# Order of the first loads of a SwiGLU feed-forward kernel: everything on SyncE's queue, x in two pieces

## The chip, the cores and the metric

The kernel runs on one core of a Trainium2 chip. The metric is the device time of one execution in microseconds. Three runs of the kernel before gave 120.56, 121.11 and 121.32 us, so its median is 121.11 us. One more execution was taken with the hardware profiler; all views below are of that one.

## The reference

```python
B, S, D, F = 1, 2048, 512, 1376          # bf16 throughout
def reference(x, w_gate, w_up, w_down):
    g = jax.nn.silu(x @ w_gate)          # [2048, 512] @ [512, 1376]
    u = x @ w_up
    return (g * u) @ w_down              # [2048, 1376] @ [1376, 512]
```

## The kernel before

TensorE (PE) contracts over partitions, so x is needed with D on the partitions: the tile xT_sb holds x transposed, four blocks of 128 of D by 2048 tokens. Tokens go in four chunks of 512. F is cut into ten full tiles of 128 columns and a rest of 96. For each chunk and each F tile PE makes a gate product and an up product (four matmuls each, one per block of D, out to one PSUM bank of 128x512, line 327). ScalarE (ACT) takes SiLU of the gate bank into sg_sb (line 279), VectorE (DVE) multiplies it with the up bank into hT_sb (line 288). After all chunks PE makes the down product from hT_sb and the w_down tile wd_sb (line 392), DVE copies each row block to o_sb (line 292), and SyncE (SP) stores it. The rest of 96 columns has matmuls of its own (lines 368, 379 and 406).

The work of every engine is one list written out by hand; semaphores join them. PE's list sets the order. Each matmul group waits, through need(name), for the loads that it reads, and through after(engine, n) for the n-th operation of ACT or DVE.

The change touches the start alone, which runs like this.

- **Transposed x.** Chunks 1 to 3 and the second half of chunk 0 (tokens 256 to 511, the load x0b) come through transposing DMAs straight into xT_sb (line 86). The first 256 tokens come as a plain load, xn (line 107), into xn_sb, and PE transposes them: two token tiles i = 0, 1, each in two halves h = 0, 1 of D, each half two 128x128 transposes (line 344) into its own PSUM bank. DVE copies the halves h = 0 to xT_sb, ACT the halves h = 1. Here tile i holds every second token, since xn puts two neighbouring tokens on one partition; rows_of undoes this when the output rows are stored.
- **Loads.** ACT issues the gate and the up weights of F tile 0 ahead of its first work (line 91). SP issues xn, the gate and up weights of F tile 1, x0b, and then the rest in slabs of F tiles (2, 3), (4 to 6), (7 to the end), the other chunks of x, and w_down.
- **PE.** Five dummy matmuls of 512 columns on constants (line 336, N_WARM) run first. Then PE waits for the identity and for xn, makes the eight transposes, and then, for F tiles 0 and 1 of chunk 0 (gate g0, up u0, gate g1, up u1): g0 on tokens 0 to 127, g0 on 128 to 255, u0 likewise, g1 and u1 on tokens 0 to 255, and then all four on tokens 256 to 511, which need x0b. From F tile 2 on every matmul has 512 columns.

Of the kernel before, what the change touches and what calls it, by code (L numbers as in the profile page):

```python
# [7 lines left out]
FP32 = mybir.dt.float32  # L8

N_WARM = 5  # L10


def bass_standalone__swiglu_ffn__prompt_kernel(nc, x, w_gate, w_up, w_down, out):
    _, S, D = x.shape
    F = w_gate.shape[1]
    P = 128
    KD = D // P
    NFF = F // P
    NFT = NFF + 1
# [8 lines left out]
    HT = SC // 2  # L28
    NXN = HT // P
# [5 lines left out]
    xf = x[0]  # L35
    of = out[0]


    UPH = F + 32
# [4 lines left out]
    with ExitStack() as es:  # L44
# [16 lines left out]
        o_sb = [sb(f"o_sb{i}", [P, D], BF16) for i in range(NOS)]  # L61
        banks = [ps(f"bank{i}", [P, 512], FP32) for i in range(NB)]

        xn_sb = sb("xn_sb", [P, NXN, D], BF16)
# [8 lines left out]
        s_out = [sem(f"s_out{i}") for i in range(NOS)]  # L73
        loads = {}

        def load_sem(name):
            loads[name] = sem(f"s_{name}")
            return loads[name]
# [6 lines left out]
        def load_x(eng, name, t0, t1):  # L85
            eng.dma_start_transpose(
                xT_sb[:, :, t0:t1], xf[t0:t1, :]
            ).then_inc(load_sem(name), 16)

        def load_w(eng, name, src, base, f0, f1):  # L90
            eng.dma_start(
                w_sb[:, :, base + f0:base + f1],
                src[:, f0:f1].rearrange("(k p) f -> p k f", p=P),
            ).then_inc(load_sem(name), 16)

        slabs = [(0, 1), (1, 2), (2, 4), (4, 7), (7, NFT)]
        slab_of = {ft: a for a, b in slabs for ft in range(a, b)}

        def load_slab(eng, a, b):
            load_w(eng, f"wg{a}", w_gate, 0, a * P, min(b * P, F))  # L100
            load_w(eng, f"wu{a}", w_up, UPH, a * P, min(b * P, F - 32))

        def loads_on_scalar(act):
            load_slab(act, *slabs[0])

        def loads_on_sync(sp):
            sp.dma_start(
                xn_sb[:, :, :].rearrange("p j d -> p (j d)"), xf[0:HT, :].rearrange("(p j) d -> p (j d)", j=NXN)
            ).then_inc(load_sem("xn"), 16)
            load_slab(sp, *slabs[1])  # L110
            load_x(sp, "x0b", HT, SC)
            for a, b in slabs[2:]:
                load_slab(sp, a, b)
            load_w(sp, "wut", w_up, F - (F - 32), F - 32, F)
            for c in range(1, NSC):
                load_x(sp, f"x{c}", c * SC, (c + 1) * SC)
            sp.dma_start(
                wd_sb[:, 0:NFF, :], w_down[0:NFF * P, :].rearrange("(k p) d -> p k d", p=P)
            ).then_inc(load_sem("wd"), 16)
            for c in range(NSC):  # L120
                sp.dma_start(
                    wdt_sb[R * c:R * (c + 1), :, :], w_down[NFF * P:F, :].rearrange("(q p) d -> p q d", p=R)
                ).then_inc(load_sem(f"wdt{c}"), 16)
            sp.dma_start(wdl_sb[:, :], w_down[NFF * P:F, LASTA:D]).then_inc(load_sem("wdl"), 16)
# [7 lines left out]
        def add_group(kind, **what):  # L132
            g = dict(kind=kind, at=len(groups), bank=banks[len(groups) % NB], readers=[], **what)
            groups.append(g)
            return g
# [8 lines left out]
        def tview(bank):  # L144
            return bank[:, 0:P].bitcast(BF16).rearrange("p (k t) -> p k t", k=2)
# [61 lines left out]
        for i in range(NXN):  # L207
            for h, eng in enumerate("DA"):
                g = add_group("T", i=i, h=h)
                op = add_op(  # L210
                    eng, g, kind="copy", out=xT_sb[:, 2 * h:2 * h + 2, i * P:(i + 1) * P],
# [15 lines left out]
        for at in range(NST):  # L227
            j, c = divmod(at, NSC)
            t = c * TPC + j
            ob = at % NOS  # L230
            need = 16 * n_store[ob]
            halves = [(0, D)] if at < NST - 1 else [(0, LASTA), (LASTA, D)]
            for c0, c1 in halves:
                g = add_group("O", t=t, c0=c0, c1=c1, c=c)
                if c0 == 0:
                    quads[j].append(g)
                else:
                    last = g
                eng = "A" if len(halves) == 2 and c0 == 0 else "D"
                op = add_op(  # L240
                    eng, g, kind="copy", out=o_sb[ob][:, c0:c1], src=g["bank"][:, 0:c1 - c0],
# [3 lines left out]
                n_store[ob] += 1  # L245


        def rows_of(t):
            if t < NXN:
                return of[0:HT, :].rearrange("(p j) d -> j p d", j=NXN)[t]  # L250
            return of[t * P:(t + 1) * P, :]

        def on_sync(sp):
            loads_on_sync(sp)
            for t, c0, c1, ob, eng, n in stores:
                sp.wait_ge(s_A if eng == "A" else s_D, n)
                sp.dma_start(rows_of(t)[:, c0:c1], o_sb[ob][:, c0:c1]).then_inc(s_out[ob], 16)
            for i in range(NOS):
                sp.wait_ge(s_out[i], 16 * n_store[i])

# [3 lines left out]
            ).then_inc(s_I, 1)  # L264

        def on_scalar(act):
            loads_on_scalar(act)
            act.activation(adummy[:, 0:4], zero_c, ACT.Silu)  # L268
            for op in act_ops:
                act.wait_ge(s_P, op["g"]["at"] + 1)  # L270
                if op["kind"] == "silu":
                    if op["free"]:
                        act.wait_ge(s_D, op["free"])
                    fn = ACT.Silu
                else:
                    if op["stored"][1]:
                        act.wait_ge(*op["stored"])
                    fn = ACT.Copy
                act.activation(op["out"], op["src"], fn).then_inc(s_A, 1)  # L279
# [15 lines left out]
        def on_tensor(pe):  # L295
            landed = set()

            def need(name):
                if name not in landed:
                    pe.wait_ge(loads[name], 16)  # L300
                    landed.add(name)
# [3 lines left out]
            def after(eng, n):  # L305
                if n > read[eng]:
                    pe.wait_ge(s_A if eng == "A" else s_D, n)
                    read[eng] = n
# [6 lines left out]
            def gu_matmuls(g, n0, n1):  # L315
                c, ft = g["c"], g["ft"]
                if c > 0:
                    need(f"x{c}")
                if c == 0 and n1 > HT:
                    need("x0b")  # L320
                need(("wg" if g["kind"] == "G" else "wu") + str(slab_of[ft]))
                col = (0 if g["kind"] == "G" else UPH) + ft * P
                for dk in range(KD):
                    if c == 0 and dk % 2 == 0:
                        for i in range(n0 // P, min(n1 // P, NXN)):
                            after(*xt_ready[i, dk // 2])
                    ins = pe.matmul(  # L327
                        g["bank"][:, n0:n1], lhsT=w_sb[:, dk, col:col + P],
                        rhs=xT_sb[:, dk, c * SC + n0:c * SC + n1], start=(dk == 0), stop=(dk == KD - 1),
                    )  # L330
                if n1 == SC:
                    ins.then_inc(s_P, 1)

            def warm(n, width):
                for i in range(n):
                    pe.matmul(banks[NB - 1][:, 0:width], lhsT=ones_w, rhs=ones_m[:, 0:width], start=True, stop=True)  # L336

            warm(N_WARM, SC)
            pe.wait_ge(s_J, 1)
            need("xn")  # L340
            for g in groups[:NT]:
                for k in range(2):
                    dk = 2 * g["h"] + k
                    ins = pe.transpose(tview(g["bank"])[:, k, :], xn_sb[:, g["i"], dk * P:(dk + 1) * P], ident[:, :])  # L344
                ins.then_inc(s_P, 1)

            g0, u0, g1, u1 = groups[NT:NT + 4]
            for g in (g0, u0):
                gu_matmuls(g, 0, P)
                gu_matmuls(g, P, HT)  # L350
            gu_matmuls(g1, 0, HT)
            gu_matmuls(u1, 0, HT)
            for g in (g0, u0, g1, u1):
                gu_matmuls(g, HT, SC)
# [73 lines left out]
            t, c0, c1 = last["t"], last["c0"], last["c1"]  # L428
# [3 lines left out]
            ).then_inc(s_P, 1)  # L432

        on_sync(nc.sync)
        on_gpsimd(nc.gpsimd)
        on_scalar(nc.scalar)
        on_tensor(nc.tensor)
        on_vector(nc.vector)

# [27 lines left out]
```

## Time and profile before

| | us |
|---|---|
| median of three runs | 121.11 |
| the profiled execution | 120.31 |
| its span, first to last instruction | 119.0 |
| PE busy | 115.6 (97%) |
| DVE busy | 47.2 (40%) |
| ACT busy | 31.0 (26%) |
| first transpose on PE | 3.71 |
| first matmul of line 327 | 4.56 |

A PE that is busy need not run at its best: the records of matmuls overlap, so the spacing of their starts tells the speed. A matmul of 512 columns starts every 0.216 us in the long middle part of this kernel, and every 0.427 us among the first dummies. An instruction that issues a DMA is listed under its engine with a q (SPq, ACTq) and its time is that of issuing; the time to landing runs from the start of the issue until the semaphore has its full count.

### The profile page before, as it was taken

Reading aid. Unit: us, or ns where it says so; the run is one execution under the profiler, and the core shown is the slowest. Engines: PE = TensorE matmul, PEld = TensorE weight load, DVE = VectorE, ACT = ScalarE, POOL = GpSimd, SP = SyncE. Lnnn points to the kernel's source line nnn. Section 1 sums busy time; section 2 is a strip of 40 time slices with the busy share of each in tenths; the row PEclk is TensorE's granted clock in tenths of the full one; section 3 lists DMA queues with packets and bytes.
Section 4 is the critical chain, followed back from the end, with each engine's and each line's share of the span. In section 5 each row is a group of like instructions: output and inputs, shape, how many; then the busy total and the mean of one; then the engine's idle time right before and its main releaser. Section 6 shows DMA issues by size and latency. Waiting matters only on the chain.

```text
span 119.0 us, 1524 instructions
## 1 busy us (share of the span) xinstructions
PE 115.6 (97%) x608; PEld 53.7 (45%) x608; DVE 47.2 (40%) x73; ACT 31.0 (26%) x53; POOL 0.4 (0%) x5
## 2 busy tenths in 40 slices
PE   7799999999999999999999999999999999999993
PEld 1674444444444444444444444444434444444452
DVE  0133443353433444433444334469617422006530
ACT  4344324453234363244262343230000000000001
POOL 1000000000000000000000000000000000000000
PEclk9999999999999999999999999999999999999999
DMA  3999999990000000000000000000004221002412
GB/s 90 277 299 365 265 101 272 307 254 10 0 0 0 6 0 0 0 0 6 0 0 0 6 0 0 0 0 0 0 0 138 88 88 44 0 0 76 150 44 88
DMA packets 17559, 8.84 MB, mean 74 GB/s; under 512 B 10640, under 2 KB 17424, under 8 KB 17552
## 3 DMA queue, kind: packets, MB, share of 16 engines
q1 hardware_dynamic: 16496, 8.48, 27.8%
q10 hardware_dynamic: 1056, 0.26, 1.0%
q8 instruction: 5, 0.08, 0.3%
q14 instruction: 2, 0.02, 0.0%
HBM read 4.81 MB, written 2.10 MB: 58 GB/s over the span
## 4 chain that ended last, share of the span: by engine, by line
PE 95%; DMA 2%; DVE 0%; issue 0%
PE bank L327 58%; PE bank L392 29%; PE bank L368 3%; DMA xn_sb<-in_x_dram 2%; PE bank L406 2%; PE bank L379 2%; PE bank L344 1%; DVE o_sb L292 0%; PE bank L429 0%
## 5 line engine op out<-in xcount | busy, mean ns | idle before, releaser
L327 PE MATMUL bank<-xT_sb,w_sb 128*128 128x512 bf16 (+2 forms) x344 | 70.0, 364 | 0.0
L327 PEld LDWEIGHTS bank<-xT_sb,w_sb 128*128 128x128 bf16 x344 | 32.8, 98 | 36.3
L288 DVE TENSOR_TENSOR hT_sb<-sg_sb,bank 128x512 bf16<-128x512 f32 x40 | 27.5, 688 | 40.4 <-PE bank L327 36.6
L392 PE MATMUL bank<-wd_sb,hT_sb 128*128 128x512 bf16 (+2 forms) x170 | 35.1, 367 | 0.0
L279 ACT ACTIVATE sg_sb<-bank 128x512 f32<-128x512 f32 x40 | 23.8, 596 | 40.7 <-PE bank L327 40.7
L392 PEld LDWEIGHTS bank<-wd_sb,hT_sb 128*128 128x128 bf16 x170 | 16.0, 98 | 19.1 <-issue 1.3
L292 DVE CAST o_sb<-bank 128x512 bf16<-128x512 f32 (+1 forms) x16 | 10.1, 663 | 22.0 <-PE bank L406 12.3
L279 ACT ACTIVATE o_sb<-bank 128x384 bf16<-128x384 f32 x1 | 0.5, 490 | 37.8 <-PE bank L392 37.8
L288 DVE TENSOR_TENSOR ht_sb<-sgy_sb,bank 32x512 bf16<-32x512 f32 x8 | 5.5, 683 | 0.2
L288 DVE TENSOR_TENSOR ht_sb<-sgx_sb,bank 32x512 bf16<-32x512 f32 x4 | 2.8, 692 | 3.5 <-ACT sgx_sb L279 3.5
L368 PE MATMUL bank<-xT_sb,w_sb 128*128 128x512 bf16 x16 | 4.1, 379 | 0.0
L279 ACT ACTIVATE sgx_sb<-bank 32x512 f32<-32x512 f32 x4 | 2.3, 587 | 4.5 <-PE bank L368 4.5
L336 PE MATMUL bank<-const-bfloat16-1.0 128*128 128x512 bf16 x5 | 2.3, 621 | 0.8 <-PEq L452 0.8
L406 PE MATMUL bank<-wdt_sb,ht_sb 32*128 32x512 bf16 (+1 forms) x48 | 2.9, 372 | 0.0
L368 PEld LDWEIGHTS bank<-xT_sb,w_sb 128*128 128x128 bf16 x16 | 1.6, 98 | 1.9
L279 ACT ACTIVATE sgy_sb<-bank 64x512 f32<-64x512 f32 x4 | 2.4, 590 | 0.1
L379 PE MATMUL bank<-xT_sb,w_sb 128*64 128x512 bf16 x16 | 1.9, 382 | 0.0
L406 PEld LDWEIGHTS bank<-wdt_sb,ht_sb 32*128 32x128 bf16 x48 | 1.1, 92 | 1.7 <-issue 0.8
L268 ACT ACT_TABLE_LOAD x1 | 1.3, 1283 | 1.8 <-issue 1.8
L292 DVE COPY xT_sb<-bank 128x256 bf16<-128x256 bf16 x2 | 0.6, 292 | 2.9 <-PE bank L344 2.8
L344 PE MATMUL bank<-ident,xn_sb 128*128 128x128 bf16 x8 | 0.8, 275 | 0.6 <-DMA xn_sb<-in_x_dram 0.6
L344 PEld LDWEIGHTS bank<-ident,xn_sb 128*128 128x128 bf16 x8 | 0.7, 130 | 1.5 <-issue 1.5
(14 smaller groups left out, 4.0 us busy)
## 6 DMA issues: line engine op xcount, KB each, us to landing
out_dram<-o_sb SPq DMA_DIRECT2D x15, 128.0 KB, 1.7
wd_sb<-in_w_down_dram SPq DMA_DIRECT2D x1, 1280.0 KB, 8.0
w_sb<-in_w_gate_dram SPq DMA_DIRECT2D x1, 480.0 KB, 6.0
w_sb<-in_w_up_dram SPq DMA_DIRECT2D x1, 448.0 KB, 6.6
w_sb<-in_w_gate_dram SPq DMA_DIRECT2D x1, 384.0 KB, 4.7
w_sb<-in_w_up_dram SPq DMA_DIRECT2D x1, 384.0 KB, 5.2
wdt_sb<-in_w_down_dram SPq DMA_DIRECT2D x4, 96.0 KB, 6.8
xn_sb<-in_x_dram SPq DMA_DIRECT2D x1, 256.0 KB, 2.8
```

The costliest lines, as they stand in the source:

```text
L268: act.activation(adummy[:, 0:4], zero_c, ACT.Silu)
L279: act.activation(op["out"], op["src"], fn).then_inc(s_A, 1)
L288: ins = dve.tensor_tensor(op["out"], op["a"], op["b"], ALU.mult)
L292: ins = dve.tensor_copy(op["out"], op["src"])
L327: ins = pe.matmul(g["bank"][:, n0:n1], lhsT=w_sb[:, dk, col:col + P], rhs=xT_sb[:, dk, c * SC + n0:c * SC + n1], start=(dk == 0), stop=(dk ...
L336: pe.matmul(banks[NB - 1][:, 0:width], lhsT=ones_w, rhs=ones_m[:, 0:width], start=True, stop=True)
L344: ins = pe.transpose(tview(g["bank"])[:, k, :], xn_sb[:, g["i"], dk * P:(dk + 1) * P], ident[:, :])
L368: ins = pe.matmul(g["bank"][:, :], lhsT=w_sb[:, dk, XC0:XC0 + P], rhs=xT_sb[:, dk, c * SC:(c + 1) * SC], start=(dk == 0), stop=(dk == KD - 1),
L379: ins = pe.matmul(g["bank"][y0:y1, :], lhsT=w_sb[:, dk, YC0:YC0 + 64], rhs=xT_sb[:, dk, c * SC:(c + 1) * SC], start=(dk == 0), stop=(dk == ...
L392: ins = pe.matmul(g["bank"][:, 0:c1 - c0], lhsT=hT_sb[:, fk, t * P:(t + 1) * P], rhs=wd_sb[:, fk, c0:c1], start=(start and fk == 0), stop= ...
L406: ins = pe.matmul(g["bank"][:, 0:c1 - c0], lhsT=ht_sb[R * c:R * (c + 1), q, j * P:(j + 1) * P], rhs=wdt_sb[R * c:R * (c + 1), q, c0:c1], s ...
```

## The change

- All early loads are issued by SP, none by ACT. Their order is: piece 0 of x (128 tokens, xn0), the gate weights of F tiles 0 and 1 in one load (wg0, 256 columns), piece 1 of x (xn1), the up weights of both tiles in one load (wu0), then x0b and the slabs as before.
- The pieces of x are plain tiles of 128 tokens, so rows_of goes away.
- PE runs two dummies of 128 columns more ahead of the wait (N_FILL), waits for each piece of x by itself, and runs four dummies of 128 columns (N_WAIT) between the transposes of piece 0 and the wait for piece 1.
- The first matmuls are reordered: g0 and g1 on tokens 0 to 127, g0 and g1 on tokens 128 to 255, u0 and u1 on tokens 0 to 255, then all four on tokens 256 to 511.

```diff
+N_FILL = 2
+N_WAIT = 4
...
-        slabs = [(0, 1), (1, 2), (2, 4), (4, 7), (7, NFT)]
+        slabs = [(0, 2), (2, 4), (4, 7), (7, NFT)]
...
-        def loads_on_scalar(act):
-            load_slab(act, *slabs[0])
+        def load_xn(eng, i):
+            eng.dma_start(xn_sb[:, i, :], xf[i * P:(i + 1) * P, :]).then_inc(load_sem(f"xn{i}"), 16)
 
         def loads_on_sync(sp):
-            sp.dma_start(
-                xn_sb[:, :, :].rearrange("p j d -> p (j d)"), xf[0:HT, :].rearrange("(p j) d -> p (j d)", j=NXN)
-            ).then_inc(load_sem("xn"), 16)
-            load_slab(sp, *slabs[1])
+            load_xn(sp, 0)
+            load_w(sp, "wg0", w_gate, 0, 0, slabs[0][1] * P)
+            load_xn(sp, 1)
+            load_w(sp, "wu0", w_up, UPH, 0, slabs[0][1] * P)
             load_x(sp, "x0b", HT, SC)
-            for a, b in slabs[2:]:
+            for a, b in slabs[1:]:
                 load_slab(sp, a, b)
...
-        def rows_of(t):
-            if t < NXN:
-                return of[0:HT, :].rearrange("(p j) d -> j p d", j=NXN)[t]
-            return of[t * P:(t + 1) * P, :]
...
         def on_scalar(act):
-            loads_on_scalar(act)
             act.activation(adummy[:, 0:4], zero_c, ACT.Silu)
...
             warm(N_WARM, SC)
+            warm(N_FILL, P)
             pe.wait_ge(s_J, 1)
-            need("xn")
             for g in groups[:NT]:
+                if g["i"] > 0 and g["h"] == 0:
+                    warm(N_WAIT, P)
+                need(f"xn{g['i']}")
                 for k in range(2):
...
             g0, u0, g1, u1 = groups[NT:NT + 4]
-            for g in (g0, u0):
-                gu_matmuls(g, 0, P)
-                gu_matmuls(g, P, HT)
-            gu_matmuls(g1, 0, HT)
+            for n0, n1 in ((0, P), (P, HT)):
+                gu_matmuls(g0, n0, n1)
+                gu_matmuls(g1, n0, n1)
+            gu_matmuls(u0, 0, HT)
             gu_matmuls(u1, 0, HT)
             for g in (g0, u0, g1, u1):
                 gu_matmuls(g, HT, SC)
```

More of the change, by code (lines that the diff above doesn't have):

```diff
@@ L256, in on_sync @@
                 sp.wait_ge(s_A if eng == "A" else s_D, n)
-                sp.dma_start(rows_of(t)[:, c0:c1], o_sb[ob][:, c0:c1]).then_inc(s_out[ob], 16)
+                sp.dma_start(of[t * P:(t + 1) * P, c0:c1], o_sb[ob][:, c0:c1]).then_inc(s_out[ob], 16)
             for i in range(NOS):
```

## The prediction

> **What bounds the kernel now.** I read the chain that ended last first, since it tells in which stretch a change can count at all.
>
> ```profile
> 0.74 2.83 DMA xn_sb<-in_x_dram
> 3.58 0.14 issue
> 3.71 0.85 PE bank L344 x8
> 4.56 17.66 PE bank L327 x104
> ...
> 23.08 17.27 PE bank L327 x80
> ```
>
> Columns: start, length, what. From 3.71 us to 117 us the chain is PE alone, so the end moves only by what moves PE's start or opens a hole behind it. The first chunk's 104 matmuls hold the columns of the 80 in a later chunk and take 17.66 - 17.27 = 0.39 us more. Second, the issues in order of time and the times to landing (last number).
>
> ```profile
> 0.73 0.46 ACTq L91 DMA_DIRECT2D w_sb<-in_w_gate_dram  x1
> 0.74 0.39 SPq L107 DMA_DIRECT2D xn_sb<-in_x_dram  x1
> 1.19 0.41 SPq L91 DMA_DIRECT2D w_sb<-in_w_gate_dram  x1
> ...
> 2.20 1.77 SPq L86 DMA_TRANSPOSE xT_sb<-in_x_dram  x1
> 4.02 0.58 SPq L91 DMA_DIRECT2D w_sb<-in_w_gate_dram  x1
> ```
>
> ```profile
> xn_sb<-in_x_dram SPq DMA_DIRECT2D x1, 256.0 KB, 2.8
> w_sb<-in_w_gate_dram SPq DMA_DIRECT2D x1, 256.0 KB, 3.5
> w_sb<-in_w_up_dram SPq DMA_DIRECT2D x1, 256.0 KB, 3.7
> w_sb<-in_w_up_dram SPq DMA_DIRECT2D x1, 128.0 KB, 3.8
> out_dram<-o_sb SPq DMA_DIRECT2D x15, 128.0 KB, 1.7
> ```
>
> xn lands at 0.74 + 2.83 = 3.57 and the first transpose starts 0.13 later. The last up load ahead of x0b lands at 1.66 + 3.8 = 5.4. The same list cut to 2 to 4 us gives x0b 4.2 us, so it lands at 6.4. The matmuls that need it start at 6.49: **x0b has 0.05 us to spare**. Third, the busy times by stretch (PE, PEld, DVE, ACT, POOL, granted clock, DMA share, GB/s).
>
> ```profile
> 0.77:3.06 2.29, 2.29 (x5) 0.55 (x5) 0.23 (x1) 1.28 (x1) 0.23 (x1) 1.00 0.47 129
> 3.06:3.71 0.65, 0.00 (x1) 0.03 (x1) 0.00 (x0) 0.21 (x2) 0.00 (x0) 1.00 1.23 277
> ...
> 1.75:2.50 0.75, 0.75 (x4) 0.15 (x1) 0.00 (x0) 0.72 (x1) 0.00 (x0) 1.00 0.68 145
> 2.50:3.50 1.00, 0.56 (x2) 0.00 (x0) 0.00 (x0) 0.77 (x2) 0.00 (x0) 1.00 1.09 307
> 3.50:4.75 1.25, 1.04 (x10) 0.83 (x10) 0.56 (x2) 0.42 (x2) 0.00 (x0) 1.00 1.28 286
> 4.75:5.75 1.00, 1.00 (x18) 0.92 (x17) 0.03 (x1) 0.24 (x1) 0.00 (x0) 1.00 1.29 273
> ```
>
> PE's hole of 0.65 us lies between dummies and transposes, and the DMA engines are full from 2.5 us on: what is asked for first comes first, and the rest waits for bytes. The clock column says 1.00 throughout, but transposes start 0.107 us apart up to 4.2 us and 0.055 us apart after 4.3, so PE doubles its speed near 4.25 us.
>
> **Piece 0 of x.** xn0 is half of xn and issued at the same 0.74. Bounds for its landing: 2.44 (the 128 KB store's 1.7 us) and 3.57 (nothing gained). 128 KB less at 307 GB/s is 0.4 us, so I take 3.2. The dummies end at 3.06 + 2 x 0.107 = 3.27. Transposes of piece 0: from 3.33, four at 0.107, to 3.76. The four waiting dummies: to 4.19. All this gains nothing by itself, since PE then waits for piece 1.
>
> **Piece 1 of x decides.** Ahead of xn1's last byte stand xn0, wg0 and xn1: 512 KB (524 thousand bytes). Before, the engines had moved 0.75 x 145 = 109 by 2.50, 109 + 307 = 416 by 3.50, and 524 at 3.5 + 108/286 = 3.88. Semaphores follow the bytes: 768 KB (786) were through at 4.75 + 13/273 = 4.80 and the last up load landed at 5.4, a lag of 0.6. So xn1 lands near 4.45. Its own issue agrees: xn0 takes SP to 1.19, wg0 some 0.5 to 1.69, and 1.69 + 2.8 (xn's row) = 4.49. Low end: 415 thousand bytes after 2.50 at the 365 GB/s of the page's fourth slice (8.9 to 11.9 us, rows of 768 bytes and more), 3.64, with a lag of 0.4: 4.05. High end: wg0 lands 3.5 after its issue at 1.19 as the row of 256 KB does, 4.69, and xn1 another 131/307 = 0.4 later: 5.1. I take 4.45, on which two ways agree.
>
> **The first matmuls.** Before, the last transpose started at 4.34 and the x0b matmuls at 6.49, 2.15 later; that held three waits for copies of transposes, read from the starts (0.217, 0.158 and 0.098 us apart where 0.055 is the pace): 0.16 + 0.10 + 0.04 = 0.30 us. In the new order piece 0 is copied long before, so the first two waits go. Piece 1's ACT copy was ready 5.05 - 4.34 = 0.71 after the last transpose; now 0.055 + 8 x 0.056 + 2 x 0.056 = 0.62 lies in front of the matmul that needs it: a wait of 0.09. Gain 0.30 - 0.09 = 0.2 us. Matmul count and columns stay (104).
>
> So, with xn1 at L: transposes from L + 0.13, the last at L + 0.30, the x0b matmuls at L + 0.30 + 2.15 - 0.21 = L + 2.24. **Break-even with 6.49 is L = 4.25.** With 4.45: +0.2 us. Ends: 4.05 gives -0.2, 5.1 gives +0.85.
>
> **The other loads.** wu0 closes the same 768 KB, so 5.4; it is wanted at L + 1.3 = 5.8 (nothing; issued at 2.14, its 3.7-us row gives 5.84, also next to nothing). x0b's bytes again come behind 768 KB, but its issue moves from 2.20 to about 2.68, since SP now carries two 256-KB weight loads and one x issue more in place of two of 128 KB. Bound by bytes it lands at 6.4 and hides before 6.69. Bound by its issue it lands at 2.68 + 4.2 = 6.9: 0.2 us. I take bytes: the engines show no free share ahead of it. The DMA row first (two queues, together 286 GB/s), then the rule: by the Trainium skill, "DMA: Bandwidth & Descriptors", section "Issuing engines are not separate DMA queues", a second issuing engine saves only issue time, no bandwidth. That speaks against this change: it would give that saving up, and by it x0b is at 6.4 while bytes bind and at 6.9 where issuing does; no run shown here tells which.
>
> Later slabs move by 0.5 us in issue: (2, 3) landed at 4.02 + 3.5 = 7.5 and is wanted at 8.24, so the cover holds even then. ACT loses two issues and loads its table earlier, ending at 3.06 now and first needed at 4.33: nothing. The plain output rows are the same 128 KB stores.
>
> **The clock.** The two and four dummies shrink the hole of 0.65 us. PE sped up 3.5 us after its first dummy in spite of that hole, so nothing is gained in this execution. The three timed runs lie 0.25 to 1.0 us above it; if that is a later rise of the clock (each microsecond later costs half of it), a denser start might bring some of it forward. Bounds: 0 and 0.8 us (all of the median's excess, 121.11 - 120.31); I take 0.1, near the end that the row shows.
>
> **Sum.** 120.31 + 0.2 - 0.1 = 120.4 us for an execution like the profiled one. The median stands 0.8 above, so 121.11 + 0.1 = **121.2 us, no change that can be told**: about 1%, or 1.2 us, is what a measurement of this kernel can tell.
>
> **The rivals.**
> - *Bytes come sooner and the clock earlier.* Larger pieces run faster (L = 4.05, -0.2) and the filled hole gives back half of the excess (-0.4): 120.5 us. For it: 256-byte rows become 512-byte rows, 308 GB/s where those of 512 bytes flow (6.5 to 7.75) against 286. Against: the clock rose despite the hole. Chance 0.22.
> - *SP's queue is the new limit: slower.* wg0 and xn1 are bound by issue and latency, not bytes: L = 5.1, x0b matmuls at 7.34 (x0b at 6.9 already there): +0.85, 121.9 to 122.0. It decides once L passes 4.25, and shows as a PE hole ahead of piece 1's transposes, which dummies end too early to cover (4.19). For it: one sequencer issues what two did. Against: bytes flowed at 273 to 307 GB/s from 2.5 us on, so issue was ahead of them. Chance 0.18.
> - *It does not bring x forward.* The first 1.0 us to the first bytes is fixed and xn0 lands at 3.57: transposes to 4.13, dummies to 4.56, piece 1 then from 4.56, L in effect 4.43: as forecast, 121.2. It is counted there.
> - *The clock is a matter of phase.* Row: speed doubles at 4.25. If it can rise anywhere within the next 3.4 us, each run has its own cold stretch and filling changes nothing: up to 1.7 us on single runs, 121.3 at the median (the +0.2 alone). The rule beside it: the Trainium skill, "TensorE: Matmul & The Clock Gate", Part 1, has a free-running window of 3413 ns. The trace agrees with its length (3.5 us after the first dummy); one execution cannot show its phase. Chance 0.15.
>
> **How the numbers follow.** Forecast 0.45, rivals 0.22, 0.18 and 0.15. The forecast and the phase rival lie within 1%. Faster by over 1% means under 119.9, the first rival with all of the 0.8: 0.08. Slower by over 1% means over 122.3, the second with a later clock: 0.10. The rest, 0.82, is within. The range reaches to both outer rivals, 120.4 to 122.0.
>
> **What would show it.** In the profile after: first transpose near 3.3; the second four near 4.6, with a DMA wait of xn_sb of 0.3 to 0.4 us ahead of them; the starts behind without the gaps of 0.217 and 0.158; x0b matmuls near 6.7 and unbroken; x0b's time to landing down to about 3.7 to 3.9. The forecast falls if x0b or wu0 ends a wait of PE for over 0.3 us, if piece 1 starts before 4.2 or after 5.1, or if the middle chunks (17.27 us) change.

## The result and the profile after

The kernel after takes 121.37 us at the median of 20 runs (121.15 to 121.56); the kernel before, run 20 times beside it, 120.62 us (120.30 to 121.90). The ratio, formed over all runs (the two medians alone give 1.006), is 1.0043, 95% interval 1.0026 to 1.0059: slower by 0.4%, within the 1% that was called no change. The profiled execution took 121.54 us, its span is 120.1 us; before it was 120.31 and 119.0.

The chain of work that ended last in the kernel after (start, length, what):

```profile
1.66 0.50 SPq L106
2.16 0.04 issue
2.20 4.33 DMA w_sb<-in_w_up_dram
6.53 0.04 issue
6.58 2.96 PE bank L323 x24
```

Before, the chain came to PE at 3.71 us by way of xn. Now it runs through SP's own issues and the up load wu0, which takes 4.33 us from its issue and holds PE until 6.58.

SP's issues of the kernel after in order of time, and PE's work beside them:

```profile
0.74 0.40 SPq L106 DMA_DIRECT2D xn_sb<-in_x_dram  x1
1.20 0.41 SPq L93 DMA_DIRECT2D w_sb<-in_w_gate_dram  x1
1.66 0.50 SPq L106 DMA_DIRECT2D xn_sb<-in_x_dram  x1
2.20 0.43 SPq L93 DMA_DIRECT2D w_sb<-in_w_up_dram  x1
2.68 1.57 SPq L88 DMA_TRANSPOSE xT_sb<-in_x_dram  x1
```

```profile
3.07 0.63 PE L343 MATMUL bank<-ident,xn_sb 128*128 128x128 bf16 x4
3.50 0.63 PE L332 MATMUL bank<-const-bfloat16-1.0 128*128 128x128 bf16 x4
4.60 0.61 PE L343 MATMUL bank<-ident,xn_sb 128*128 128x128 bf16 x4 [0.47 <-DMA xn_sb<-in_x_dram]
5.00 1.39 PE L323 MATMUL bank<-xT_sb,w_sb 128*128 128x128 bf16 x16
6.58 1.65 PE L323 MATMUL bank<-xT_sb,w_sb 128*128 128x256 bf16 x12 [0.18 <-DMA w_sb<-in_w_up_dram]
```

The transposes of piece 0 start at 3.07, of piece 1 at 4.60, the first matmul at 5.00 (4.56 before), the first on wu0 at 6.58. The matmuls that need x0b start at 7.61 in the trace, 6.49 before. That is 1.12 us, and the span grew by 1.1: all that was lost was lost ahead of this point.

The stretches that tell why (PE, PEld, DVE, ACT, POOL, granted clock, DMA share, GB/s), first of the kernel after, then of the kernel before:

```profile
2.50:3.00 0.50, 0.50 (x4) 0.23 (x3) 0.00 (x0) 0.00 (x0) 0.00 (x0) 1.00 0.71 131
3.00:4.00 1.00, 1.00 (x11) 0.86 (x9) 0.29 (x1) 0.26 (x1) 0.00 (x0) 1.00 1.04 308
4.00:6.50 2.50, 1.93 (x22) 1.62 (x20) 0.29 (x1) 0.51 (x2) 0.00 (x0) 1.00 1.04 170
```

```profile
2.50:3.00 0.50, 0.50 (x2) 0.00 (x0) 0.00 (x0) 0.50 (x1) 0.00 (x0) 1.00 0.97 333
3.00:4.00 1.00, 0.35 (x5) 0.32 (x5) 0.00 (x0) 0.27 (x2) 0.00 (x0) 1.00 1.24 284
4.00:6.50 2.50, 2.50 (x32) 2.02 (x31) 0.58 (x2) 0.66 (x2) 0.00 (x0) 1.00 1.21 264
```

From 4.0 to 6.5 us the DMA engines moved 170 GB/s in place of 264. Their share did not fall as far, since pieces (the packets of a load, one by one in the trace) stood inside the engines. A piece of 512 bytes goes through in 27 ns as a rule; ten of those begun between 3.98 and 5.01 us took 250 to 830 ns. More time went into 17 pieces of x0b, which stood until 6.39 us, as the last section shows.

### The profile page after: what moved, and what is told of

Read it like the earlier page. It is cut to its first block, busy times and chain, and to the rows that moved or that the text cites. A ratio compares the mean times of both kernels' runs of the same rounds, so it can differ in the third digit from the quotient of the medians.

```text
span 120.1 us, 1524 instructions
## 1 busy us (share of the span) xinstructions
PE 116.0 (97%) x603; PEld 54.9 (46%) x614; DVE 47.3 (39%) x73; ACT 31.1 (26%) x53; POOL 0.4 (0%) x5
## 4 chain that ended last, share of the span: by engine, by line
PE 92%; DMA 4%; SPq 1%; issue 1%; DVE 0%
PE bank L323 57%; PE bank L391 29%; DMA w_sb<-in_w_up_dram 4%; PE bank L367 3%; PE bank L405 2%; PE bank L378 2%; SPq L106 1%; SPq L93 0%; DVE o_sb L288 0%; PE bank L428 0%
## 5 line engine op out<-in xcount | busy, mean ns | idle before, releaser
L323 PEld LDWEIGHTS bank<-xT_sb,w_sb 128*128 128x128 bf16 x344 | 33.3, 99 | 36.5 <-DMA w_sb<-in_w_up_dram 0.4
L391 PE MATMUL bank<-wd_sb,hT_sb 128*128 128x512 bf16 (+2 forms) x166 | 34.5, 366 | 0.4 <-issue 0.3
L332 PE MATMUL bank<-const-bfloat16-1.0 128*128 128x128 bf16 (+1 forms) x11 | 3.1, 455 | 0.8 <-PEq L451 0.8
L367 PEld LDWEIGHTS bank<-xT_sb,w_sb 128*128 128x128 bf16 x16 | 1.6, 98 | 1.9
L332 PEld LDWEIGHTS bank<-const-bfloat16-1.0 128*128 128x128 bf16 x11 | 1.4, 143 | 2.1 <-issue 2.1
```

Source lines behind the costliest of these rows:

```text
L323: ins = pe.matmul(g["bank"][:, n0:n1], lhsT=w_sb[:, dk, col:col + P], rhs=xT_sb[:, dk, c * SC + n0:c * SC + n1], start=(dk == 0), stop=(dk ...
L367: ins = pe.matmul(g["bank"][:, :], lhsT=w_sb[:, dk, XC0:XC0 + P], rhs=xT_sb[:, dk, c * SC:(c + 1) * SC], start=(dk == 0), stop=(dk == KD - 1),
L391: ins = pe.matmul(g["bank"][:, 0:c1 - c0], lhsT=hT_sb[:, fk, t * P:(t + 1) * P], rhs=wd_sb[:, fk, c0:c1], start=(start and fk == 0), stop= ...
```

## The experiments

Each kernel is the kernel after but for the edit shown, unless it says otherwise. Landings are from the trace.

**Which of the loads' changes costs the time.**

```diff
 # e1_weights_on_act
         def loads_on_sync(sp):
             load_xn(sp, 0)
-            load_w(sp, "wg0", w_gate, 0, 0, slabs[0][1] * P)
             load_xn(sp, 1)
-            load_w(sp, "wu0", w_up, UPH, 0, slabs[0][1] * P)
...
         def on_scalar(act):
+            load_w(act, "wg0", w_gate, 0, 0, slabs[0][1] * P)
+            load_w(act, "wu0", w_up, UPH, 0, slabs[0][1] * P)
```

> The kernel after, with wg0 and wu0 issued by ACT again; SP issues xn0, xn1, x0b. Theory A (one queue at the start is short of issue or descriptors, so two queues fill the DMA engines): 270 GB/s or more between 4.0 and 6.5 us in place of some 170, wu0 landed by 5.5 us in place of 6.5, x0b by 6.5 in place of 7.6, no wait of PE for either over 0.2 us, and a time about 0.8 us under the kernel after (near that of before, 120.5). Theory B (the transposing load, once it is queued, slows the plain loads in flight, whatever queue they are on): wu0 lands at 6.3 or later and the time stays within 0.3 us of the kernel after (121.1 to 121.6).

Measured: 120.47 us (ten runs), ratio to before 0.998 (0.996 to 1.001). wu0 landed at 5.3, x0b at 6.4, and PE waited for neither. The stretches of this kernel:

```profile
3.00:4.00 1.00, 1.00 (x11) 0.76 (x9) 0.29 (x1) 0.50 (x3) 0.00 (x0) 1.00 1.12 353
4.00:6.50 2.50, 2.10 (x29) 1.89 (x29) 0.29 (x1) 0.54 (x2) 0.00 (x0) 1.00 1.21 276
```

Moving two loads back to ACT returns the whole loss, with the pieces of x, the 256-column loads, the dummies and PE's order all kept.

```diff
 # e2_x0b_plain: tokens 256 to 511 are not transposed
-            load_x(sp, "x0b", HT, SC)
+            sp.dma_start(
+                xT_sb[:, :, HT:SC], xf[HT:SC, :].rearrange("(p j) (k d) -> p (j k) d", j=2, k=2)
+            ).then_inc(load_sem("x0b"), 16)
```

> The kernel after, with the transposing load x0b replaced by a plain load of the same 256 KB to the same place in rows of 512 bytes; the transposition of tokens 256 to 511 is left out, so the values for these tokens are not those of the reference. Theory A (one queue is too little at the start): the stretch from 4.0 to 6.0 us stays near 170 GB/s and wu0 lands at 6.3 to 6.6 us as before. Theory B (the transposing load slows its neighbours): 290 GB/s or more in that stretch, wu0 lands at 5.2 to 5.5, x0b by 6.4, and the time falls by 0.7 to 1.0 us against the kernel after.

Measured: 121.38 us, ratio 1.005 (1.003 to 1.007). wu0 landed at 6.7. The stretch from 4.0 to 6.5, and the last two half microseconds of it:

```profile
4.00:6.50 2.50, 2.23 (x22) 1.93 (x20) 0.29 (x1) 0.51 (x2) 0.00 (x0) 1.00 0.94 220
5.50:6.00 0.50, 0.50 (x8) 0.50 (x6) 0.00 (x0) 0.00 (x0) 0.00 (x0) 1.00 1.08 321
6.00:6.50 0.50, 0.49 (x7) 0.31 (x5) 0.00 (x0) 0.00 (x0) 0.00 (x0) 1.00 1.06 285
```

The transposing load is not what makes wu0 late. It is part of the low rate, though: in the last two rows the kernel after moved 142 and 122 GB/s, and this one 321 and 285. And without it wu0 landed engine by engine, on the first of the 16 at 5.05 us and on the last at 6.68, and PE waits for the last. (SP is done with the plain x0b sooner, so the slabs behind it are issued 0.9 us earlier than in the kernel after; that difference is not separated.)

**The two halves of the change.** First the kernel before with PE's part, then the kernel after without its order of matmuls.

```diff
 # e3_pe_part_alone (edit of the kernel before)
             warm(N_WARM, SC)
+            warm(2, P)
...
-            for g in (g0, u0):
-                gu_matmuls(g, 0, P)
-                gu_matmuls(g, P, HT)
-            gu_matmuls(g1, 0, HT)
+            for n0, n1 in ((0, P), (P, HT)):
+                gu_matmuls(g0, n0, n1)
+                gu_matmuls(g1, n0, n1)
+            gu_matmuls(u0, 0, HT)
             gu_matmuls(u1, 0, HT)
 # e4_loads_alone: the same four lines turned back in the kernel after
```

> The kernel before with its loads as they are, and of the change only PE's two dummies more and the order g0, g1, then u0, u1. By the prediction two waits for copies go (0.2 us), but x0b lands at 6.4 us and was wanted at 6.49, so PE gains 0.05 us and then waits for x0b: the same time as before within 0.2 us (120.4 to 120.8). If it is slower than before by over 0.5 us, the order of the matmuls and not the loads is what made the kernel after slower.

> The kernel after with the order of the matmuls of before (g0, u0, g1, u1); loads, pieces and dummies as after. If the late loads decide, u0 is wanted sooner and waits for wu0 (6.5 us) with g1 still undone, so the matmuls that need x0b start near 7.9 in place of 7.6: 0.2 to 0.4 us over the kernel after (121.6 to 121.8). If PE's order had cost something, it falls below 121.2.

Measured: e3 120.72 us, ratio 0.999 (0.995 to 1.002), no change, x0b at 6.44 as before. e4 122.43 us, ratio 1.013 (1.005 to 1.021). Two of its four runs, 121.67 and 121.75, are as expected; the other two, 123.12 and 123.33, are slower by more. The profiled execution is the one of 123.12: its waits in PE say only 0.5 us, and the rest is PE's speed, which doubled at 9.7 us in place of 5.7. PE's order costs nothing. That in the kernel after it keeps the late wu0 from costing more is pointed to by e4, but its interval overlaps that of the kernel after, so it is not shown.

**What starves the engines.** wu0 was late whether or not a transposing load stood behind it. Is it w_up, the row of 512 bytes, a first access, or the place in the queue?

```diff
 # e5_swap: wu0 second, wg0 fourth
             load_xn(sp, 0)
-            load_w(sp, "wg0", w_gate, 0, 0, slabs[0][1] * P)
+            load_w(sp, "wu0", w_up, UPH, 0, slabs[0][1] * P)
             load_xn(sp, 1)
-            load_w(sp, "wu0", w_up, UPH, 0, slabs[0][1] * P)
+            load_w(sp, "wg0", w_gate, 0, 0, slabs[0][1] * P)
 # e6_narrow_one_queue
-            load_w(sp, "wg0", w_gate, 0, 0, slabs[0][1] * P)
+            load_w(sp, "wg0", w_gate, 0, 0, P)
+            load_w(sp, "wg1", w_gate, 0, P, 2 * P)
             load_xn(sp, 1)
-            load_w(sp, "wu0", w_up, UPH, 0, slabs[0][1] * P)
+            load_w(sp, "wu0", w_up, UPH, 0, P)
+            load_w(sp, "wu1", w_up, UPH, P, 2 * P)
 # e7_touch_up; e8_touch_down has w_down[0:512, 0:32]
         def on_scalar(act):
+            act.dma_start(
+                touch[:, :, :], w_up[:, 0:32].rearrange("(k p) f -> p k f", p=P)
+            ).then_inc(s_touch, 16)
```

> The kernel after with wu0 second and wg0 fourth in SP's order; PE's list is as after, so g0 waits for the fourth load and the time is of no use; the landings are. In the kernel after, single pieces of the fourth load took 340 to 830 ns in place of 27, and it landed at 6.5 us. Theory C (the first reads of w_up are slow, wherever they stand): the second load lands at 4.7 or later (4.2 after) and the fourth at 5.7 or earlier. Theory D (the fourth load on a queue that runs nearly empty is slow, whatever it reads): second load at 4.0 to 4.4, fourth at 6.3 to 6.7.

> The kernel after with each of the two 256-KB weight loads cut into two of 128 KB (rows of 256 bytes as before the change), all still on SP: xn0, wg0, wg1, xn1, wu0, wu1, x0b. If the row of 512 bytes is what is slow at the start, the 768 KB ahead of x0b are through by 4.9 us and the last up load lands by 5.6. If one queue is too little whatever the rows (theory D), the last up load lands at 6.3 or later, x0b at 7.5 or later, and the time is 121.3 to 122.0 us.

> The kernel after, and at its start ACT issues one small load more, 64 bytes of each of the 512 rows of w_up into a tile that nobody reads (32 KB in all). Theory C (first reads of w_up are slow): the small load takes the slow reads early, beside xn0 and wg0, and wu0 lands at 5.7 or earlier, x0b at 6.7 or earlier, the time falls by 0.6 us or more against the kernel after. Theory D (one nearly empty queue is slow at each new load): wu0 still lands at 6.3 or later, the time stays within 0.3 us of the kernel after.

> The control of the run before it: the small load on ACT reads 64 bytes of 512 rows of w_down, which nothing reads in this stretch. Theory C: no gain, wu0 at 6.3 or later. Theory D: the same as the run before it. If both small loads bring wu0 to 5.7 or earlier, it is the second queue as such that helps, not what it reads.

Measured: in e5 (one run, 123.51 us) the second load landed at 4.05, the fourth at 6.33: the place decides, not the tensor. In e6 (122.17 us, four runs; ratio 1.012, 1.003 to 1.022) the last up load landed at 6.5 and x0b at 7.6, so rows of 256 bytes do not mend it; the two extra issues put that load's issue at 3.22 in place of 2.20, so this speaks less clearly than e5. In e7 (ratio 1.003, 1.000 to 1.007) wu0 landed at 6.1 and x0b at 7.25; in its control e8 (one run, 121.5 us) at 6.3 and 7.5. Against 6.5 and 7.6 after, a first read taken early is worth some 0.2 us over the control, not the 0.8 that theory C asked for. Executions with the very loads of the kernel after differ by as much: wu0 at 6.36 in e4, 6.37 in e11.

e6 shows the pace of a single queue best. Its issues and their times to landing:

```profile
xn_sb<-in_x_dram SPq DMA_DIRECT2D x2, 128.0 KB, 2.3
w_sb<-in_w_gate_dram SPq DMA_DIRECT2D x2, 128.0 KB, 2.4
```

SP issues one every 0.5 us and each lands some 2.4 us behind its issue (3.57, 4.16, 4.68, 5.15 us). 131 thousand bytes per 0.5 us is 262 GB/s at best, and the last load, wu1, fell behind even that (3.3 us from issue to landing).

**Second queue or early issue?** In e1 the weights are on a second queue and are also issued sooner (0.73 and 1.22 in place of 1.20 and 2.20).

```diff
 # e9_act_late (edit of e1): the two loads behind ACT's first activation
+            act.activation(adummy[:, 0:4], zero_c, ACT.Silu)
             load_w(act, "wg0", w_gate, 0, 0, slabs[0][1] * P)
             load_w(act, "wu0", w_up, UPH, 0, slabs[0][1] * P)
-            act.activation(adummy[:, 0:4], zero_c, ACT.Silu)
 # e12_wu0_late_on_act (edit of e1)
             load_w(act, "wg0", w_gate, 0, 0, slabs[0][1] * P)
+            act.activation(adummy[:, 0:4], zero_c, ACT.Silu).then_inc(s_W, 1)
+            act.wait_ge(s_W, 1)
             load_w(act, "wu0", w_up, UPH, 0, slabs[0][1] * P)
-            act.activation(adummy[:, 0:4], zero_c, ACT.Silu)
```

> The first experiment (wg0 and wu0 on ACT's queue) with both issued only after ACT has loaded its table, so at about 2.2 and 2.8 us in place of 0.7 and 1.2, later than SP issues them in the kernel after (1.20 and 2.20). If the second queue is what helps, the engines stay full and wu0 lands by 5.8, x0b (issued at 1.66) by 6.5. If a load lands some 4.1 to 4.3 us behind its issue whatever the queue, so that the early issue is what helps, wu0 lands at 6.7 to 7.1 and the matmuls that need x0b start near 7.6: a time of 121.2 to 121.8 us.

> The first experiment again, with wu0 on ACT's queue issued only after ACT's first dummy activation has ended, which the run of late issue on ACT failed to do (its loads still went out at 0.79 and 1.26): wg0 at 0.7, wu0 at about 2.7, later than the 2.20 at which SP issues it in the kernel after. If the second queue is what helps, wu0 lands within 3.3 us of its issue, by 6.0, and x0b by 6.5 to 6.7; time 120.4 to 120.9 us. If issuing early is what helps, wu0 lands 4.1 us or more behind its issue, at 6.8 or later, x0b at 7.6 or later, and the time is 121.2 us or more.

e9 did not do what it set out to: ACT still issued at 0.79 and 1.26, so it is e1 once more and says nothing on lateness (120.65 us; ratio 0.996, 0.992 to 1.000). e12 did, in the execution whose trace is kept: wu0 was issued at 2.75 and landed at 8.70. Its issue rows, then its PE waits:

```profile
w_sb<-in_w_up_dram ACTq DMA_DIRECT2D x1, 256.0 KB, 6.0
xT_sb<-in_x_dram SPq DMA_TRANSPOSE x1, 5.8
```

```profile
PE bank L325 <- DMA w_sb<-in_w_up_dram: 2.7, 1, 2.7
```

Four runs took 122.70, 124.07 and twice 126.0 us; the ratio, 1.022 (1.014 to 1.031), is of the first two. The trace is of one of 126.0 us, in which PE's clock was halved for a while (last section), so its landing at 8.70 stands for that execution alone. Here a second queue did not help a load that was issued late, and did not fill the engines: they moved 129 GB/s between 3.82 and 7.20 us (row in the last section), less than the one queue of the kernel after. The run is not a clean test, though: x0b was issued at 1.66, ahead of wu0, and its pieces went through from 3.57 on, wu0's from 4.53. How much of the 6.0 us is lateness and how much the transposing load beside it stays open.

```diff
 # e10_x0b_second (edit of e3): weights of F tiles 0 and 1 in one load each on ACT
-        slabs = [(0, 1), (1, 2), (2, 4), (4, 7), (7, NFT)]
+        slabs = [(0, 2), (2, 4), (4, 7), (7, NFT)]
...
-            load_slab(sp, *slabs[1])
             load_x(sp, "x0b", HT, SC)
-            for a, b in slabs[2:]:
+            for a, b in slabs[1:]:
```

> A candidate: x's first 256 tokens in one load as before, x0b right behind it on SP (issued at 1.2), the gate and up weights of F tiles 0 and 1 in one load each on ACT (0.7 and 1.2), PE in the order g0, g1, u0, u1. If early issue decides, x0b lands at 1.2 + 4.7 = 5.9 and wu0 at 5.3, the matmuls that need x0b start near 6.2 in place of 6.49, and the time is 0.2 to 0.4 us under before. If bytes decide, 1 MB is through no sooner than before: x0b or wu0 at 6.2 to 6.4, and the time equals before within 0.2 us.

Measured: 120.84 us (twelve runs), ratio 0.997 (0.994 to 1.000). x0b was issued at 1.19, 1.0 us sooner than before, and landed at 6.47 all the same, 5.3 us behind its issue. For the transposing load early issue was worth nothing here. wu0, the last of the 768 KB beside it, landed at 5.41 as the last up load did before, and x0b 1.06 us behind it: the second half of what was expected, that bytes decide.

**The dummies.**

```diff
 # e11_no_new_dummies
-            warm(N_FILL, P)
...
-                if g["i"] > 0 and g["h"] == 0:
-                    warm(N_WAIT, P)
```

> The kernel after without its two and four new dummies. By the landings PE waits for wu0 until 6.5 and for x0b until 7.6 whatever it does before, so the time is that of the kernel after within 0.2 us (121.2 to 121.6) as long as PE's speed doubles before some 6.5 us. If the dummies are what keeps the clock, the speed doubles later and single runs reach 122 us and more.

Measured: 122.04 us (ten runs, 121.33 to 122.82), ratio 1.007 (1.004 to 1.011). wu0 and x0b landed at 6.4 and 7.4, so the landings did not move, but PE did. PE's matmuls by form, 5.6 to 8 us, of e11 and then of the kernel after (busy time, mean ns of one):

```profile
L323 PE MATMUL bank<-xT_sb,w_sb 128*128 128x128 bf16 x14 | 1.7, 314 | 0.0
L323 PE MATMUL bank<-xT_sb,w_sb 128*128 128x256 bf16 x6 | 1.5, 421 | 0.0
```

```profile
L323 PE MATMUL bank<-xT_sb,w_sb 128*128 128x256 bf16 x12 | 1.6, 274 | 0.2 <-DMA w_sb<-in_w_up_dram 0.2
L323 PE MATMUL bank<-xT_sb,w_sb 128*128 128x128 bf16 x13 | 1.1, 242 | 0.0
```

In e11 matmuls of 256 columns still run at half speed (421 ns, 0.213 us apart) where the kernel after runs them at 274 ns. In this execution PE waited for neither wu0 nor x0b any more: it reached both after they had landed. The run points to the dummies being worth keeping while PE waits for piece 1; the two intervals (1.004 to 1.011, and 1.003 to 1.006 of the kernel after) overlap, so it is not settled.

## Why the prediction was right, and where it was not

The forecast was 121.2 us, no change that can be told; 121.37 us and a ratio of 1.0043 are that. It was right in the class, but that it came so close at the median is luck. The forecast was a change of +0.1 us on 121.11, the median of three runs; measured are +0.75 us on 120.62, the median of 20. A loss that was set too low by 0.65 and a base that was too high by 0.49 nearly offset each other. For an execution like the profiled one the forecast had 120.4, and the profiled one after took 121.54 us.

- **Piece 0 of x**: landing forecast 3.2, measured 2.76 (2.0 us from issue). As it said, this gained nothing: PE waited for piece 1.
- **Piece 1 of x**: forecast 4.45, measured 4.56; its transposes 4.58 against 4.60. The step held by way of SP's issue (1.69 + 2.8 forecast, 1.66 + 2.90 measured). That the sum over bytes agreed is luck: the last piece of xn1 ended at 4.25 where 3.88 was worked out, and the semaphore followed 0.3 us behind it where 0.6 had been taken. The transposes ran at half speed, since the clock rose later than in the execution before, so the first matmul came at 5.00 and not at 4.80.
- **The first matmuls**: the waits for copies are gone. Between 5.00 and 6.18 the starts are 0.107 us apart up to the clock's rise and 0.056 behind it.
- **The other loads, the step that failed**: "Bound by bytes it lands at 6.4 and hides before 6.69 ... I take bytes: the engines show no free share ahead of it." The row behind it was of two queues. With all early loads on SP the engines moved less (170 GB/s in place of 264), and wu0 landed at 6.53 where 5.4 was forecast, x0b at 7.57 where 6.4 was. PE stood 0.40 us from start to start ahead of u0 and 0.26 ahead of the x0b matmuls, where 0.056 and 0.109 are the pace. The sum had +0.2 us up to the x0b matmuls, all of it for piece 1 and nothing for these loads; measured are +1.1. Two of the prediction's own signs failed with it: the x0b matmuls, "near 6.7 and unbroken", started at 7.61, and x0b's time to landing, "down to about 3.7 to 3.9", was 4.89. By the rule of the Trainium skill that the prediction weighed here ("DMA: Bandwidth & Descriptors", section "Issuing engines are not separate DMA queues") x0b was to land between 6.4 and 6.9; 7.57 is beyond both. That ACT's issues save SP time, as the rule says, agrees with e1, where x0b was issued at 1.66 and not at 2.68. Whether more than issue time hung on them is not shown: in e1 wu0 was also issued 1.0 us sooner, and it landed 1.2 us sooner.
- **The rival of SP's queue** looked at the right place and had nearly the price (+0.85), but put it at piece 1, which came on time. Whether its mechanism, issue and latency, is the right one stays open: SP had finished issuing wu0 at 2.63 us. Its chance of 0.18 was too low: the note against it, that bytes flow at 273 to 307 GB/s from 2.5 us on, was read from the kernel that still had ACT's two issues.
- **The clock**: the prediction gave it -0.1 us. By medians the loss is 0.75 us; the two profiled executions differ by 1.23 us, their spans by 1.1. The profiled execution before was among the fastest of its kind, with the clock up at 4.25; the 20 runs of before spread over 1.6 us, those after over 0.4. A PE that waits for wu0 and x0b until 7.6 loses little to a clock that rises anywhere before that. This reading is argued from the trace; e11, where the clock rose later and the spread came back (121.3 to 122.8), agrees.

What is shown: the loss comes with moving wg0 and wu0 to SP (e1 undoes it), not with the transposing load, the tensor, PE's order or the dummies, and hardly with the row length. Nor is it that x0b takes the engines from wu0: in the kernel after 456 of its 1024 pieces ended ahead of wu0's last piece, and in e1, where nothing was late, 416. What stays open: why single pieces stand for 0.25 to 0.83 us, and how far early issue and a second queue each count, since e1 changed both. No version clearly beats the kernel before: e1, e9 and e10 are between 0.2 and 0.4% under it, with intervals that reach 1 or end within 0.0004 of it.

## What to carry to other kernels

A GB/s row of a stretch says what the engines did with the issuers and the issue times that they had. Do not carry it over to a kernel that issues in another way: here 264 GB/s became 170 when two loads moved to the other issuer, although SP had issued the last of them at 2.63 us. Landing time by landing time, ask which load ends last after the change, not only which one the change is for. And when one profiled execution is among the fastest of a spread, make the sum for the median by itself: a new wait can swallow the spread.

## What the runs showed of the hardware

**Pieces of the transposing load stand and end together.** In the kernel after, pieces of x0b go through from 4.67 us on; then 17 of them, begun between 5.23 and 6.21 us, last until between 6.34 and 6.39, all ending together, 0.2 us behind the last piece of wu0 (6.17) and as wu0 landed (6.37 on its first engine, 6.53 on its last). Between 4.0 and 6.5 us they took 11.7 of the 40 us that 16 engines have there. In e1 14 pieces ended together between 5.14 and 5.17, 0.2 us behind wu0's last piece (4.96) and just ahead of its landing (5.20 to 5.31). x0b landed some 1.05 us behind wu0 in both. That these pieces wait for wu0 is read from the times; no run changed that alone, and e12 does not fit it: there pieces of x0b stood until 4.4 and again until 5.7 us, and wu0 landed from 7.0 to 8.7.

**The clock moves in steps of 3.41 us.** In e12 the records have PE's clock up at 3.82 us, halved from 7.23 on, 1.4 us after the start of PE's last matmul ahead of its wait (5.79), and up again at 14.05 (the granted clock is the third number from the right):

```profile
3.82:7.20 3.38, 1.60 (x23) 1.17 (x21) 0.29 (x1) 0.69 (x2) 0.00 (x0) 1.00 1.16 129
7.24:14.05 6.81, 5.30 (x25) 3.76 (x26) 0.69 (x1) 1.19 (x2) 0.00 (x0) 0.50 1.14 351
14.06:24.00 9.94, 9.94 (x47) 4.48 (x46) 4.13 (x6) 3.34 (x6) 0.00 (x0) 1.00 1.15 250
```

3.41 and 6.83 us are one and two times the window of 3413 ns that the Trainium skill gives in "TensorE: Matmul & The Clock Gate", Part 1; the trace agrees. So do the clock records of the other traces: from its rise to its fall behind the kernel's end the full clock lasts 116.05 us before, after and in e1, 34 times 3.413, and 112.64 in e4, 33 times. Together they show what the prediction's phase rival could not: the rise came at 4.25 (before), 3.79 (e1), 5.7 (after) and 9.7 us (e4), with nearly the same dummies ahead of it. Less whole windows these are 0.84, 0.38, 2.28 and 2.85 us, so the phase is another in each execution. How long PE must work in a window is not settled: by its busy time 2.76 us of 3.41 were enough before, and 2.76 in e4 between 2.85 and 6.26 were not.
